# Padding the contraction of two transform stages to 128 rows in a Fourier mixing and two-layer kernel

## The chip, the core and the metric

One core of a Trainium2 chip runs the whole program. The metric is the device time of one execution in microseconds (us); the lower the better. Five engines work side by side: TensorE (PE; its weight loads are listed apart as PEld), VectorE (DVE), ScalarE (ACT), GpSimd (POOL) and SyncE (SP), which here only issues transfers. A matmul on PE multiplies a stationary tile (rows x up to 128 columns, loaded by a weight load) with a moving tile (the same rows x the columns streamed, at most 512 here); "94*128 94x512" in the profile means 94 rows by 128 stationary columns, with 512 columns streamed.

## The reference

The first half is a Fourier mixing along the sequence of 3008 positions, the second a two-layer network with a leaky rectifier. Shapes: x is 8 x 3008 x 256, the filters 1505 x 256, the two weights 256 x 2048 and 2048 x 256.

```python
X = np.fft.rfft(x, axis=1)
Y = X * (filt_r + 1j * filt_i)[None, :, :]
y = np.fft.irfft(Y, n=x.shape[1], axis=1)      # 8 x 3008 x 256
t = y.reshape(8 * 3008, 256)
h = t @ w_in
out = np.maximum(0.01 * h, h) @ w_out          # 24064 x 256, float32
```

## The kernel before

**The transform.** A sequence of 3008 is taken as 94 x 32 (`N1`, `N2`). For one batch there are four stages, each a set of matmuls in fp16 with sums in fp32 in PSUM:

- stage 1 (`s1_group`, line 259): a transform of length 94 along `n1`. The stationary tile is `fwd1` (94 of its 128 rows are in use, the rest are zero), the moving tile two of the 32 columns `n2` of `x_sb`, each with 256 channels: 16 matmuls of 94 rows x 512 columns for one batch. `x_sb` has 128 partitions; its rows 94 and up hold nothing that the transform needs. A load of x writes 96 rows (`R1`), in the last batch 94.
- stage 2 (`s2_group`, line 308) and the products with the filter (lines 314 to 323), which run on DVE and POOL; on the way the two halves of the partitions are swapped by transfers on SP's queue (lines 318 and 319).
- stage 3 (`sa_group`, line 330): the first inverse stage, 12 matmuls of 128 rows x 512 columns for one batch.
- stage 4 (`sb_group`, line 351): the inverse along `n1`. The stationary tile is `z2`, the moving tile a slice of the constant `i1_sb` with 94 columns. Both have `K4` = 96 rows in use. One batch takes 16 groups of four matmuls with 96 rows x 94 columns; ACT copies each group into `yt` (line 341).

Between stages 1 and 2 and between 3 and 4 the data is turned by way of DRAM (`dz1`, `dz2`): a store from `st1` or `st2`, a load into `z1` or `z2` (`t1_load`, `t2_load`). `z1`, `z2`, `st1` and `st2` are halves of the large tiles `big[1]` and `big[2]`, so rows 96 to 127 of `z2` keep what an earlier use of `big[1]` left there.

**The first batch** goes another way: its stages are written out as a list of steps in the string `FIRST` (the helpers `s1p`, `s2p`, `sap`, `sbp` and others), its stage 1 is line 379 and its stage 4 line 442, and turns are done by transposes on DVE. `xc` (`round_x`, line 464) rounds the first six columns of x, which come by an early load in fp32, into `x_sb`. `warm` issues matmuls on an idle tile (line 373).

**The network.** The 24064 tokens go in 47 chunks of 512. The first layer (`moe1`, line 514) and its rectifier on ACT (line 519) are followed one chunk later by the second layer: the first three chunks as plain matmuls (line 681), the others in seven products of half-size blocks with sums of blocks on DVE (lines 555 and 589 and the functions around them).

**The order.** It is fixed when the program is built. Each piece of work has a due time in units of half of a pair of first-layer matmuls (`at`, `plan`, the tables `PLANS`, `AFTER`, `REST`, `DUE`), and a heap issues the pieces in that order; stages 1 to 4 of batches 1 to 7 are put between the network's matmuls of earlier batches. Semaphores make each instruction wait for what it reads and for what it overwrites.

**Constants.** `_build_np_constants` makes the transform matrices on the host; they are stored with the program and loaded. `i1_sb` is loaded twice: for the first batch with one layout (`i1_d`, 128 rows), and from about 82 us on with the layout of the other batches (`i1t_d`, 96 rows, line 719 on SP's queue).

Of the kernel before, what the change touches and what calls it, by code (L numbers as in the profile page):

```python
# [11 lines left out]
P = 128  # L12
# [7 lines left out]
N1, N2 = 94, 32  # L20
NC = 24
Q = 32
R1 = 96
# [3 lines left out]
def _build_np_constants(N):  # L27
    n1, n2 = np.arange(N1), np.arange(N2)
    h = N2 // 2

    k2 = np.concatenate([np.arange(h), np.arange(N2 - 1, h - 1, -1)])

    sg = np.where(k2 < h, 1.0, -1.0)[None, :]
    th = 2 * np.pi * np.outer(n2, k2) / N2
    co, si = np.cos(th), np.sin(th)

    fwd1 = np.zeros((P, P))
    fwd2 = np.zeros((P, NC, P))
    inv1 = np.zeros((P, N2, N1))
    inv2 = np.zeros((P, P))  # L40

    for s, (qr, qi) in enumerate(((0, 2), (1, 3))):
        k1 = NC * s + np.arange(NC)

        cr, ci = (slice(64 * i + s, 64 * i + 64, 2) for i in range(2))
        r, i = (slice(Q * q, Q * q + Q) for q in (qr, qi))
        ang = 2 * np.pi * np.outer(n1, k1) / N1
        fwd1[:N1, qr * Q : qr * Q + NC] = np.cos(ang)
        fwd1[:N1, qi * Q : qi * Q + NC] = -np.sin(ang)
        for c in range(NC):  # L50
            t = th + 2 * np.pi * n2[:, None] * k1[c] / N
            fwd2[r, c, cr], fwd2[i, c, cr] = np.cos(t), np.sin(t)
            fwd2[r, c, ci], fwd2[i, c, ci] = -np.sin(t) * sg, np.cos(t) * sg

        w = np.where((k1 == 0) | (k1 == N1 // 2), 1.0, 2.0)[:, None] / N1
        for j in n2:
            t = ang.T + 2 * np.pi * j * k1[:, None] / N
            inv1[qr * Q : qr * Q + NC, j, :] = w * np.cos(t)
            inv1[qi * Q : qi * Q + NC, j, :] = -w * np.sin(t)
        inv2[cr, r], inv2[ci, r] = co.T, -(si * sg).T  # L60
        inv2[cr, i], inv2[ci, i] = si.T, (co * sg).T
    inv2 /= N2


    inv2r = np.concatenate([inv2[:64], -inv2[:64]], axis=0)
    inv2i = np.concatenate([inv2[64:], inv2[64:]], axis=0)
    small = np.stack([fwd1, inv2, inv2r, inv2i], axis=1)

    fwd2t = fwd2.reshape(4, Q, NC, P).transpose(1, 0, 2, 3).reshape(P, NC, P)
    inv1t = inv1.reshape(4, Q, N2, N1)[:, :NC].transpose(1, 0, 2, 3).reshape(4 * NC, N2, N1)  # L70
    fwd2 = fwd2.reshape(P, FP, NC // FP, P).transpose(1, 0, 2, 3)
    return tuple(np.ascontiguousarray(t).astype(np.float16) for t in (fwd2, inv1, small, fwd2t, inv1t))

# [2 lines left out]
def kernel(  # L76
# [9 lines left out]
    nc = tc.nc  # L86
    B, N, D = x.shape
# [30 lines left out]
    )  # L118

    f2_np, i1_np, small_np, f2t_np, i1t_np = _build_np_constants(N)  # L120
    f2_d = nc.inline_tensor(f2_np, name="fwd2_const")
    i1_d = nc.inline_tensor(i1_np, name="inv1_const")
    small_d = nc.inline_tensor(small_np, name="small_const")
    f2t_d = nc.inline_tensor(f2t_np, name="fwd2t_const")
    i1t_d = nc.inline_tensor(i1t_np, name="inv1t_const")
# [3 lines left out]
    i1_sb = cpool.tile([P, N2, N1], FP16, name="i1_sb")  # L129
# [6 lines left out]
    x_sb = cpool.tile([P, N2, D], FP16, name="x_sb")  # L136
# [19 lines left out]
    def bank(kind, n, w, hold=0.75):  # L156
        if kind == "ph":
            t = wide[turn[kind] % 2]
            turn[kind] += 1
        else:  # L160
            i = min(range(len(single)), key=lambda i: frees[i])
            t, frees[i] = single[i], max(frees[i], clock["now"]) + hold
        return t[:, : n * w].rearrange("p (n w) -> p n w", n=n)
# [5 lines left out]
    def at(time, f):  # L169
        clock["n"] += 1  # L170
        heapq.heappush(work, (time, clock["n"], f))
# [4 lines left out]
    def need(*what):  # L176
        for w in what:
            assert w in issued, w

    def noted(what, f):  # L180
        f()
        issued.add(what)

    def soon(delay, f):
        at(clock["now"] + delay, f)
# [3 lines left out]
    fwd1, inv2, inv2r, inv2i = (small_sb[:, i, :] for i in range(4))  # L189
# [47 lines left out]
    K4 = 4 * NC  # L237
# [9 lines left out]
    def ring(t, half):  # L247
        v = t[:, ts(half, Q * D // 2)].rearrange("p (r n d) -> p r n d", r=4, n=4)
        return [v[:, r] for r in range(4)]

    z1, z2 = ring(big[1], 0), ring(big[1], 1)
    st1, st2, st1_more = ring(big[2], 0), ring(big[2], 1), ring(big[1], 1)

    def s1_group(b, g, copy):
        def go():
            ps = bank("pf", 2, D)
            h = g // 2
            need(("x", b, h if b > 1 else 0), *[("st1", b, h - 4)] * (h > 3 and b > 1))
            nc.tensor.matmul(ps, fwd1[:N1], x_sb[:N1, ds(2 * g, 2), :], start=True, stop=True)  # L259
            issued.add(("s1", b, g))  # L260
            st = st1[h % 4] if b > 1 or h < 4 else st1_more[h % 4]
            copy(st[:, ds(2 * (g % 2), 2), :], ps)  # L262
            if g % 2:
                soon(AFTER[0], lambda: noted(("st1", b, h), lambda: nc.sync.dma_start(
                    dz1[b % 2][ds(4 * h, 4)].rearrange("n p d -> p n d"), st)))
        return go
# [71 lines left out]
    def quad_copy(h, dt, ps, copy):  # L338

        yv = yt[:, dt, ts(h, QT)].rearrange("p (a c) -> p a c", c=4)  # L340
        copy(yv, ps.rearrange("p c a -> p a c"))  # L341

    def sb_group(b, g, copy):
        h, dt = g // 2, g % 2

        def go():
            ps = bank("pf", 4, N1)
            need(("z2", b, h), ("i1t",))
            issued.add(("sb", b, g))
            for j in range(4):  # L350
                nc.tensor.matmul(ps[:, j, :], z2[h % 4][:K4, j, ts(dt, P)], i1_sb[:K4, 4 * h + j, :],  # L351
                                 start=True, stop=True)
            quad_copy(h, dt, ps, copy)
        return go
# [108 lines left out]
    def round_x(n0, n, e):  # L463
        engine[e](x_sb[:N1, ds(n0, n), :], x_early[:N1, ds(n0, n), :])

    FIRST = """
        xc 0 4 A, xc 4 2 D, warm 18, s1p 0 0 4 b3, s1p 0 4 2 b0, warm 3, s1p 0 14 2 b1, s1e 0 4 2 D,
        s1e 0 0 4 A, s1p 0 10 4 b4, s1e 0 10 4 A, s1p 0 6 4 b3, s1e 0 14 2 D, warm 4, s1p 0 20 4 b4,
        s1e 0 6 4 D, s1p 0 16 4 b3, s1e 0 16 4 A, s1p 0 26 2 b2, s1p 0 24 2 b0, s1e 0 24 2 A, s1e 0 20 4 D,
        s1p 0 28 2 b1, s1p 0 30 2 b4, s1e 0 26 2 D, s1e 0 30 2 A, s1e 0 28 2 D, t1 0, t1 1, warm 14,  # L470
# [12 lines left out]
        sbe 0 3 D, sbe 1 0 D  # L483
    """
    steps = dict(s1p=s1p, s1e=s1e, t1=t1, s2p=s2p, s2d=s2d, s2a=s2a, s2m=s2m, sap=sap, sae=sae, t2=t2,
                 sbp=sbp, sbe=sbe, x=load_x, w_out=load_w_out, xc=round_x, warm=keep_warm)
    for step in FIRST.split(","):
        what, *args = step.split()
        steps[what](*(int(v) if v.isdigit() else v for v in args))
# [226 lines left out]
                lambda v=k1s: dve(fa_sb[64:P, v], fa_sb[0:64, v]))):  # L716
            at(TWICE[0] + TWICE[1] * (3 * i + n), f)
    at(F2T, lambda: noted(("f2t",), lambda: nc.sync.dma_start(f2_sb[:], f2t_d.ap())))
    at(26, lambda: noted(("i1t",), lambda: nc.sync.dma_start(i1_sb[:K4], i1t_d.ap())))
    for b in range(1, B):  # L720
        z = 47 * (b - 4) if b > 4 else 0
        p = PLANS[min(b, 4) - 1]
# [18 lines left out]
    while queue:  # L741
        time, n, stage, b, g, f = heapq.heappop(queue)
# [62 lines left out]
```

## Time and profile before

| What | Value |
|---|---|
| runs | 746.96, 747.57, 748.95 us; median 747.57 |
| span of the profiled execution (first to last instruction) | 745.2 us |
| PE busy, share of the span | 738.0 us, 99% |
| granted TensorE clock, mean | 0.999 |
| matmuls of line 259 (stage 1, batches 1 to 7) | 112, from 35.1 to 508.2 us |
| matmuls of line 351 (stage 4, batches 1 to 7) | 448, from 109.2 to 711.0 us |
| matmuls in all | 8017 |
| load of `i1t_d` (line 719) | one, 564 KB, issued at 82.1 us |

The program's own time is known only by the runs; the span is what the profiler saw of one execution. A busy PE says little by itself, since matmuls overlap in the array: the mean duration of one is a latency, and what counts for a stream of them is the step from the start of one to the start of the next.

### The profile page before, as it was taken

How to read it: one execution, taken by the hardware profiler on the slowest of the kernel's cores; microseconds unless marked ns; L12 is line 12 of the kernel's file. 1: busy time of each engine (PE TensorE's matmuls, PEld its weight loads, DVE VectorE, ACT ScalarE, POOL GpSimd, SP SyncE). 2: the span in 40 equal slices, each digit the busy share in tenths (PEclk: the TensorE clock that was granted, in tenths of full speed). 3: DMA queues.
4: the chain of work that ended last, by engine and by line, in shares of the span. 5: the costliest groups of instructions: out<-in, count | busy, mean ns of one | idle time of the engine just before them, and what ended most of it. 6: DMA issues, size and time to landing. Idle time of an engine off the chain costs nothing.

```text
span 745.2 us, 19416 instructions
## 1 busy us (share of the span) xinstructions
PE 738.0 (99%) x8017; PEld 528.9 (71%) x8017; DVE 504.6 (68%) x686; ACT 559.1 (75%) x755; POOL 166.2 (22%) x171
## 2 busy tenths in 40 slices
PE   9999999999999999999999999999999999999997
PEld 3556667677687777877778777777777777777776
DVE  5987637766776766766777667766677676465566
ACT  4776787888878787877777787787777777777762
POOL 6503412332232212121232222121212210000000
PEclk9999999999999999999999999999999999999999
DMA  9997797888876666655675656543554333111012
GB/s 207 229 224 197 191 224 216 209 195 208 216 181 147 159 186 176 169 138 163 193 178 150 159 155 175 156 139 109 144 160 119 106 103 103 60 55 55 29 46 70
DMA packets 119848, 113.64 MB, mean 152 GB/s; under 512 B 16384, under 2 KB 93056, under 8 KB 119568
## 3 DMA queue, kind: packets, MB, share of 16 engines
q1 hardware_dynamic: 104425, 94.73, 42.9%
q0 software_dynamic: 15056, 17.49, 15.8%
q8 instruction: 62, 1.02, 0.6%
q14 instruction: 26, 0.21, 0.1%
q10 hardware_dynamic: 279, 0.19, 0.1%
HBM read 57.51 MB, written 50.33 MB: 145 GB/s over the span
## 4 chain that ended last, share of the span: by engine, by line
PE 96%; DMA 1%; DVE 1%; ACT 1%; issue 0%; ACTq 0%; DVEq 0%
PE ph L514 43%; PE pf L589 18%; PE po_ps L589 18%; PE pf L259 3%; PE pf L351 3%; PE pf L308 2%; PE pf L330 2%; PE po_ps L373 1%; PE pf L681 1%; PE po_ps L681 1%; DMA dz<-big 1%; DMA big<-dz 0%; ACT yt L341 0%; PE pf L442 0%; PE ph L401 0%
## 5 line engine op out<-in xcount | busy, mean ns | idle before, releaser
L519 ACT ACTIVATE gt_c<-ph 128x1024 f16<-128x1024 f32 x376 | 385.3, 1025 | 133.5 <-PE ph L514 122.8
L514 PE MATMUL ph<-yt,w_in_sb 128*128 128x512 f16 (+7 forms) x1728 | 447.3, 351 | 0.2 <-ACT yt L341 0.2
L589 PEld LDWEIGHTS <-gt_c 128*128 128x128 f16 x2800 | 202.2, 98 | 91.1
L323 POOL TENSOR_TENSOR y_b_g<-p_b_g,p_b_g 128x512 f16<-128x512 f32 x84 | 116.4, 1388 | 414.9 <-DMA p_b_g<-p_b_g 249.9
L589 PEld LDWEIGHTS <-big 128*128 128x128 f16 x2128 | 151.2, 98 | 61.4
L514 PEld LDWEIGHTS <-w_in_sb 128*128 128x128 f16 x1728 | 137.5, 98 | 19.7 <-DVE yt L341 0.4
L317 DVE TENSOR_TENSOR p_b_g<-pf,fb_sb 128x512 f32<-128x512 f32 x78 | 53.7, 688 | 31.0 <-PE pf L308 13.8
L589 PE MATMUL po_ps<-wt_sb,gt_c 128*128 128x128 f16 x704 | 70.0, 219 | 0.0
L589 PE MATMUL pf<-wt_sb,gt_c 128*128 128x128 f16 x688 | 68.4, 219 | 0.0
L589 PE MATMUL pf<-w_out_sb,gt_c 128*128 128x128 f16 x720 | 67.9, 219 | 0.0
L589 PE MATMUL pf<-wt_sb,big 128*128 128x128 f16 x704 | 67.2, 219 | 0.0
L262 ACT CAST big<-pf 128x512 f16<-128x512 f32 x98 | 57.1, 588 | 11.9 <-PE pf L259 10.5
L589 PE MATMUL po_ps<-w_out_sb,gt_c 128*128 128x128 f16 x688 | 66.0, 219 | 0.0
L589 PE MATMUL po_ps<-wt_sb,big 128*128 128x128 f16 x688 | 65.3, 219 | 0.0
L341 ACT CAST yt<-pf 128x376 f16<-128x376 f32 x120 | 56.4, 473 | 10.9 <-PE pf L351 8.0
L555 DVE TENSOR_TENSOR big<-gt_c 128x2048 f16<-128x2048 f16 (+1 forms) x46 | 58.7, 1276 | 0.1
L555 DVE TENSOR_TENSOR gt_c<-gt_c 128x2048 f16<-128x2048 f16 x43 | 57.4, 1335 | 1.0
L320 DVE TENSOR_TENSOR p_b_g<-pf,fa_sb 128x512 f32<-128x512 f32 x84 | 57.2, 681 | 0.2
L555 DVE TENSOR_TENSOR big<-gt_c,big 128x2048 f16<-128x2048 f16 (+1 forms) x45 | 55.3, 1230 | 0.0
L555 DVE TENSOR_TENSOR big<-big,gt_c 128x2048 f16<-128x2048 f16 (+1 forms) x45 | 55.2, 1227 | 0.1
L332 ACT CAST big<-pf 128x512 f16<-128x512 f32 x84 | 49.0, 584 | 4.9 <-PE pf L330 3.0
L259 PE MATMUL pf<-x_sb,small_sb 94*128 94x512 f16 x109 | 41.6, 381 | 0.0
(97 smaller groups left out, 625.9 us busy)
## 6 DMA issues: line engine op xcount, KB each, us to landing
dz<-big SPq DMA_DIRECT2D x98, 256.0 KB
p_b_g<-p_b_g SPq DMA_DIRECT2D x156, 128.0 KB
out_dram<-ost_c_h SPq DMA_DIRECT2D x118, 128.0 KB
big<-dz SPq DMA_DIRECT2D x42, 256.0 KB
big<-dz SPq DMA_DIRECT2D x56, 192.0 KB
x_sb<-in_x_dram POOLq DMA_DIRECT2D x40, 192.0 KB, 4.4
x_sb<-in_x_dram POOLq DMA_DIRECT2D x2, 768.0 KB, 9.1
w_in_sb<-in_moe_w_in_dram POOLq DMA_DIRECT2D x1, 1024.0 KB, 13.2
```

Of the source, the lines that this page charges most:

```text
L259: nc.tensor.matmul(ps, fwd1[:N1], x_sb[:N1, ds(2 * g, 2), :], start=True, stop=True)
L262: copy(st[:, ds(2 * (g % 2), 2), :], ps)
L317: nc.vector.tensor_tensor(p2[:], ps, fb, AL.mult)
L320: nc.vector.tensor_tensor(p1[:], ps, fa, AL.mult)
L323: ("y", b, g), lambda: nc.gpsimd.tensor_tensor(y1[:], p1[:], p3[:], AL.add)))
L332: nc.scalar.copy(st2[h % 4][:, ds(2 * (g % 2), 2), :], ps)
L341: copy(yv, ps.rearrange("p c a -> p a c"))
L351: nc.tensor.matmul(ps[:, j, :], z2[h % 4][:K4, j, ts(dt, P)], i1_sb[:K4, 4 * h + j, :], start=True, stop=True)
L514: nc.tensor.matmul(ph[:, j, ds(t - ci * CH, e - t)], w_in_sb[:, dt, ts(ct, P)], yt[:, dt, ds(t % N, e - t)], start=(dt == 0), stop=(dt == ...
L519: nc.scalar.activation(gts[ci][:, ds(2 * g, 2), :], ph, AF.Lrelu)
L555: nc.vector.tensor_tensor(*(v[:, ds(c0, n)] for v in (o, i0, i1)), op)
L589: nc.tensor.matmul(of[t], a()[:, c, ts(t, P)], w[:, c, :], start=(c == 0), stop=(c == NCH - 1))
```

## The change

Stages 1 and 4 of batches 1 to 7 use all 128 rows of their tiles. `fwd1` has zero rows from 94 on already; the constant `inv1t` is built with zero rows from 96 on and its load brings all 128 rows. Where one factor's rows are zero, the other's must be finite: rows 96 to 127 of `x_sb` are set to zero by four memsets on DVE at the start (`blank`, 32 rows x 8 columns x 256 channels each), and rows 94 and 95 hold what the loads brought. Rows 96 to 127 of `z2` keep what was there. The first batch's own steps (lines 379 and 442) are as before.

```diff
@@ in _build_np_constants
-    inv1t = inv1.reshape(4, Q, N2, N1)[:, :NC].transpose(1, 0, 2, 3).reshape(4 * NC, N2, N1)
+    inv1t = np.zeros((P, N2, N1))
+    inv1t[: 4 * NC] = inv1.reshape(4, Q, N2, N1)[:, :NC].transpose(1, 0, 2, 3).reshape(4 * NC, N2, N1)
@@ in s1_group
-            nc.tensor.matmul(ps, fwd1[:N1], x_sb[:N1, ds(2 * g, 2), :], start=True, stop=True)
+            nc.tensor.matmul(ps, fwd1, x_sb[:, ds(2 * g, 2), :], start=True, stop=True)
@@ in sb_group
-                nc.tensor.matmul(ps[:, j, :], z2[h % 4][:K4, j, ts(dt, P)], i1_sb[:K4, 4 * h + j, :],
+                nc.tensor.matmul(ps[:, j, :], z2[h % 4][:, j, ts(dt, P)], i1_sb[:, 4 * h + j, :],
                                  start=True, stop=True)
@@ after round_x
+    def blank(i):
+        nc.vector.memset(x_sb[R1:P, ts(i, N2 // 4), :], 0.0)
+
     FIRST = """
-        xc 0 4 A, xc 4 2 D, warm 18, s1p 0 0 4 b3, s1p 0 4 2 b0, warm 3, s1p 0 14 2 b1, s1e 0 4 2 D,
+        blank 0, blank 1, blank 2, xc 0 4 A, xc 4 2 D, blank 3, warm 18, s1p 0 0 4 b3, s1p 0 4 2 b0, warm 3, s1p 0 14 2 b1, s1e 0 4 2 D,
@@ the load of the constant
-    at(26, lambda: noted(("i1t",), lambda: nc.sync.dma_start(i1_sb[:K4], i1t_d.ap())))
+    at(26, lambda: noted(("i1t",), lambda: nc.sync.dma_start(i1_sb[:], i1t_d.ap())))
```

More of the change, by code (lines that the diff above doesn't have):

```diff
@@ L485 @@
     steps = dict(s1p=s1p, s1e=s1e, t1=t1, s2p=s2p, s2d=s2d, s2a=s2a, s2m=s2m, sap=sap, sae=sae, t2=t2,
-                 sbp=sbp, sbe=sbe, x=load_x, w_out=load_w_out, xc=round_x, warm=keep_warm)
+                 sbp=sbp, sbe=sbe, x=load_x, w_out=load_w_out, xc=round_x, warm=keep_warm, blank=blank)
     for step in FIRST.split(","):
```

## The prediction, made before the changed kernel ran

> **What bounds the kernel now.** I read the page's busy times and its chain of waits first, then the matmul groups kept apart by shape, then the starts of single matmuls.
>
> ```profile
> PE 738.0 (99%) x8017; PEld 528.9 (71%) x8017; DVE 504.6 (68%) x686; ACT 559.1 (75%) x755; POOL 166.2 (22%) x171
> PE 96%; DMA 1%; DVE 1%; ACT 1%; issue 0%; ACTq 0%; DVEq 0%
> 120.00:720.00 600.00, 600.00 (x6752) 1.00 0.54 144
> ```
>
> The first line gives busy time by engine, the second the shares of the chain that ended last, the third (busy time of PE by stretches) says that from 120 to 720 us PE was busy for 600.00 of 600.00 us at full granted clock. So in that stretch the time is the sum of the steps from one matmul's start to the next; no other engine's time counts unless it makes PE wait. What the change touches there are two groups, beside a full-row one of the same width as the first:
>
> ```profile
> L259 PE MATMUL pf<-x_sb,small_sb 94*128 94x512 f16 x109 | 41.6, 381 | 0.0
> L259 PE MATMUL po_ps<-x_sb,small_sb 94*128 94x512 f16 x3 | 1.1, 379 | 0.0
> L351 PE MATMUL pf<-i_sb,big 96*128 96x94 f16 x448 | 38.1, 206 | 0.2 <-DMA big<-dz 0.2
> L330 PE MATMUL pf<-y_b_g,small_sb 128*128 128x512 f16 x84 | 31.8, 379 | 0.0
> ```
>
> The mean durations (381, 206, 379 ns) are latencies and overlap their neighbours, so they do not price anything. The price is the step, taken from the matmul start times in this trace (medians over matmuls that did not wait, ns from a start to the next start):
>
> ```
> full 128 rows, columns streamed:  64: 28.3   128: 55.9   192: 82.6   256: 109.2   320: 135.8   384: 162.7   448: 189.5   512: 216
> L259 (94 rows, 512), after a 128-row matmul:      220     the 128-column matmul behind it: 58 (undisturbed: 56)
> L330 (128 rows, 512), after a 128-row matmul:     216     the 128-column matmul behind it: 56
> L351 (96 rows, 94), first to fourth of a group:   45.7, 44.4, 44.4, 44.3     the 128-column matmul behind them: 58
> L379 (94 rows, 512), three in a row at 7.66 us:   220, 215, 215     then L373 with 128 rows: 220, 215, 215
> ```
>
> The reader should see that a matmul whose row count differs from the one before it takes some 4 ns more than its width says, that the way back costs some 2.6 ns (5 for the 512-wide L373), and that matmuls within a run of 94 rows cost nothing extra (215). Full-row steps lie on a straight line in the columns, 0.417 ns each.
>
> **The change part by part.** The order of instructions is the same on every engine, except for four memsets more on DVE; the waits are on the same engines and queues.
>
> *L259, 112 matmuls (16 in each of seven batches).* Each stands alone between full-row matmuls. Averaged over all that did not wait, the excess is 4.1 ns on its own step and 2.6 on the next. With 128 rows it is an L330: no excess. Gain 112 x 6.7 ns = 0.75 us. Bounds: 0.75, and 0 if the excess is not due to the row count.
>
> *L351, 448 matmuls in 112 groups of four.* The way back to 128 rows: 112 x 2.6 = 0.29 us. In the group, 45.7 + 44.4 + 44.4 + 44.3 = 178.8 ns. No row shows 94 columns over full rows at full width. The line of full-row widths gives 55.9 - 34 x 0.417 = 41.7 ns, so 166.8 for four: 12.0 ns x 112 = 1.34 us. This is one end. The other: 94 columns cost 44.4 whatever the rows, and only the first step's 1.3 ns goes: 0.15 us. For the first end speaks that all eight full-row widths lie on the line within 1 ns, that the excess is the same for all 32 places in i1_sb (44 to 46 ns), so not a matter of where the 94 columns start, and that the two groups that PE entered after waiting (at 109.2 and 130.5 us) made their first step in 41 and 40 ns: 94 columns can pass in 41.7. Against it speaks that L379's 94-row steps within a run show no excess, so fewer rows alone are not slow. I take the line, the nearest row for a full-row matmul, and keep 0.15 for the range.
>
> *The rows added.* The loads of the stationary side last 98 ns for 94, 96 and 128 rows alike; all lie under matmuls. The Trainium skill, in "TensorE: Matmul & The Clock Gate", section "Step-by-step: what each phase is for", says that a weight load's time follows the number of columns and that the row count does not matter. The load durations agree. By that rule alone nothing would be gained by the padding, and the time would stay at 747.6; the starts behind a change of rows speak against it.
>
> *Four memsets on DVE at the start,* 32 rows x 1024 words each. The nearest row is the memset of the same length at 1.34 us:
>
> ```profile
> 1.34 0.91 DVE L234 MEMSET big<- 128x1024 uint32 x1 [0.20 <-issue]
> 6.07 0.42 DVE L464 CAST x_sb<-big 94x512 f16<-94x512 f32 x1 [3.82 <-DMA big<-in_x_dram]
> 8.51 0.69 DVE L288 CAST big<-pf 128x512 f16<-128x512 f32 x1 [2.01 <-PE pf L379]
> ```
>
> In the timeline (start, duration, idle time before it) DVE sits idle for 3.82 us until the first input lands, and 2.01 us behind the cast. Three memsets take 3 x 0.91 = 2.73 us, or 3 x 1.09 by the other memset (0.27 for 256 words): they end between 5.0 and 5.5, before 6.07. The fourth ends by 7.6, before 8.51. Cost 0. If the cover were gone, the cast would be late; what waits for it is the third L379 matmul, at 8.09, 1.6 us after the cast's end, so up to 1.6 us of overrun costs nothing either.
>
> *The constant's load* (line 719, issued once on SP's queue) grows from 564 to 752 KB. The queue's next entries:
>
> ```profile
> 82.14 0.59 SPq L719 DMA_DIRECT2D i_sb<-inv1t_const  x1
> 85.75 1.76 SPq L575 DMA_DIRECT2D out_dram<-ost_c_t  x2
> 87.64 0.53 SPq L318 DMA_DIRECT2D p_b_g<-p_b_g  x1
> ```
>
> 188 KB at the 218 GB/s that the core moved from 80 to 120 us is 0.9 us of transfer; SP issues nothing until 85.75, and the first use is at 109.2. Should it delay the swap at 87.64 by all of the 0.9 us, the sum on POOL behind it has spare time: in that batch the sums end 3.8 to 10.3 us before PE reads them. Cost 0; without that cover 0.9 us.
>
> **Sum.** 0.75 + 0.29 + 1.34 = 2.38 us off the span, 745.2 to 742.8. The median of the runs is 747.57, 2.4 us above the span of the profiled execution; I keep that part: 747.57 - 2.38 = **745.2 us**.
>
> **The rivals.**
>
> *A, the 94 columns keep their 44.4 ns.* Gain 0.75 + 0.29 + 0.15 = 1.19: **746.4**. For it: no slow steps inside L379's runs. Against: the 40 and 41 ns after waits. Only two such steps, so nearly as likely.
>
> *B, the rows are not the cause* (what the change says does not happen on the array): the excess belongs to changing stationary tiles or buffers, and stays. **747.6**. Against: L330 and L308 change tile and buffer as well and show none.
>
> *C, slower: full-row matmuls with 94 columns run as line 442's do.* Those are the only ones in the trace (first batch, 64-column stationary halves):
>
> ```profile
> L442 PE MATMUL pf<-i_sb,big 128*64 128x94 f16 x96 | 4.9, 241 | 0.2 <-DVE big L434 0.2
> L401 PE MATMUL ph<-big,f_sb 128*64 128x128 f16 x72 | 3.0, 221 | 0.0
> ```
>
> In its group at about 64 us the pairs start some 60 to 65 ns apart, slower than the 58 mean of line 401's pairs, which are wider. If L351 took 60 instead of the 44.4 of now, it would lose 448 x 15.6 = 7.0 us, less the 1.04 us of the row changes: **753.5**. It decides against the change as soon as a step costs over 2.3 ns more than now. Against it: line 442's weights are strided and load in 157 ns where the others take 98, and the pairs follow the loads.
>
> *D, the memsets hold up POOL's transfers.* POOL writes its transfers' lists from 1.24 to 6.19 us; if it stood still for the 2.7 us of three memsets, the filter, complete at 17.33, would come at 20.1, 1.2 us after DVE's first product with it (18.86), and PE's line 425 later by as much: 1.2 us lost. With A's gain 747.6. The Trainium skill ("SBUF — State Buffer", "SBUF: two separate sides") warns that some vector instructions lock POOL out of writing descriptors. This trace shows no lock under a memset: the x load issued at 1.91, inside the 0.91 us memset of 1.34, took 0.53 us, the next one, at 2.42 without a memset, 0.52.
>
> **How the numbers follow.** Forecast 0.45, A 0.37, B 0.08, C 0.05, D 0.03, other 0.02. The three runs before span 2.0 us, so a median can be off by about 0.8; 0.3% (2.24 us) is about what can be told from no change, and the forecast's 2.38 lies hardly beyond it. Faster by more than 0.3%: 0.6 of the forecast, a tenth of A, 0.31 in all; slower: C and some of the rest, 0.06; within: 0.63. The range runs from 744.3 (forecast less 0.9) over A to 747.7, which takes in B and D; C is left out.
>
> **What would show it.** In the changed trace: the step of the L259 matmul 216 and the one behind it 56; L351's four at 41.7 (the forecast) or 44.4 (A), 60 (C), and 56 behind them; the memsets done before 6.07 and PE's wait-free stretch unchanged. The forecast is wrong if L351's step stays above 43, or if PE waits anew before 120 us.

## The result and the profile after

| | before | changed |
|---|---|---|
| median of 22 runs each | 747.58 us | 746.70 us |
| ratio changed to before | | 0.9986, 95% interval 0.998 to 0.9991 |
| span of the profiled execution | 745.2 us | 744.2 us |

The change saves 1.05 us by the ratio (0.67 to 1.50 by its interval), 0.14%: a gain clear of no change, and under half of the 2.38 us that were forecast. The time lies within the stated range (744.3 to 747.7 us) and next to rival A's 746.4, but not for A's reason, as the experiments show.

The page of the changed kernel, busy times and the chain that ended last:

```profile
PE 737.1 (99%) x8017; PEld 528.4 (71%) x8017; DVE 506.5 (68%) x690; ACT 558.9 (75%) x755; POOL 167.2 (22%) x171
PE 98%; DVE 1%; ACT 0%; issue 0%; DVEq 0%; ACTq 0%
```

PE's busy time by stretches (length, busy us, matmuls, granted clock, DMA share, GB/s):

```profile
80.00:120.00 40.00, 40.00 (x370) 1.00 0.88 221
120.00:720.00 600.00, 600.00 (x6764) 1.00 0.55 144
```

The matmul groups that were changed (busy us, mean ns of one | idle time before them):

```profile
L260 PE MATMUL pf<-x_sb,small_sb 128*128 128x512 f16 x109 | 41.3, 379 | 0.0
L352 PE MATMUL pf<-i_sb,big 128*128 128x94 f16 x448 | 37.8, 206 | 0.0
```

PE is still the bound and busy for all of the 600 us; the same 600 us now hold 12 matmuls more (6764 against 6752). The means hardly differ (379 for 381, 206 for 206), as they are latencies. The gain shows only in the starts. For each changed matmul or group the next table follows 14 steps, start to start, and gives how far each is from what its width says (columns / 2.4 + 2.5 ns, the line through the steps of the full-row matmuls: 55.9 ns for 128 columns, 216 for 512); means over the 68 to 112 places after 85 us where PE did not wait and no other changed matmul was near:

```
excess in ns                  step 0     1      2      3      4      5      6      7     sum of 14
stage 1, before (94 rows)       4.17   2.62  -0.82  -0.86  -0.78   0.00   0.11  -0.13      4.35
stage 1, changed                0.05  -0.05  -0.03   0.04  -0.05   0.02  -0.04   0.05      0.00
stage 4, before (96 rows)       4.12   2.60   2.74   2.62   2.64  -0.85  -0.84  -0.69     12.34
stage 4, changed               -0.85   4.99   2.78   2.56  -0.83  -0.85  -0.66   0.05      7.19
```

For stage 1, step 0 is the changed matmul and step 1 the one behind it; for stage 4, steps 0 to 3 are the group and step 4 the matmul behind it. Two things are to be seen. First, a stall is partly made good: the three steps behind it are 0.7 to 0.9 ns short, so a stage-1 matmul cost 4.35 ns net, not 6.7. Second, padding clears stage 1 altogether but stage 4 only in part: its first step is now free, its second is slower than before, its third and fourth are as they were.

Net, the steps give 112 x 4.35 = 0.49 us for stage 1 and 112 x (12.34 - 7.19) = 0.58 us for stage 4, together 1.06 us (with rounding): what the runs show. That the two spans differ by nearly the same, 1.04 us, is partly chance, since two other differences between the profiles cancel. The first stage-1 matmul of the first batch started 0.4 us later in the changed kernel (8.05 against 7.66 us): the warm-up matmuls ahead of it, 512 columns wide, step by 0.427 us at first and then by 0.216, which is read here as the rise of PE's clock, and that came two slow matmuls later (at 7.40 instead of 6.58 us). And PE's waits after 84 us were 0.36 us shorter (0.10 against 0.46); a wait is counted here where a step is over 20 ns longer than its width says, by what it is longer. Both vary from profile to profile of one and the same kernel, as is seen below.

DVE's timeline at the start of the changed kernel (start, duration, idle before it and what ended it):

```profile
1.34 0.91 DVE L235 MEMSET big<- 128x1024 uint32 x1 [0.20 <-issue]
2.50 0.91 DVE L468 MEMSET x_sb<- 32x1024 uint32 x1 [0.25 <-issue]
3.58 0.91 DVE L468 MEMSET x_sb<- 32x1024 uint32 x1 [0.16 <-issue]
4.65 0.91 DVE L468 MEMSET x_sb<- 32x1024 uint32 x1 [0.16 <-issue]
6.76 0.42 DVE L465 CAST x_sb<-big 94x512 f16<-94x512 f32 x1 [1.19 <-DMA big<-in_x_dram]
7.45 0.91 DVE L468 MEMSET x_sb<- 32x1024 uint32 x1 [0.27 <-issue]
8.90 0.69 DVE L289 CAST big<-pf 128x512 f16<-128x512 f32 x1 [0.54 <-PE pf L380]
```

Each memset takes 0.91 us; three are done at 5.56, and DVE still waits 1.19 us for the first input. The fourth ends at 8.36, 0.54 us before DVE has its next input. SP's queue around the larger constant; its next issue comes 3.65 us after the constant's (3.61 before):

```profile
82.39 0.56 SPq L723 DMA_DIRECT2D i_sb<-inv1t_const  x1
86.04 1.76 SPq L579 DMA_DIRECT2D out_dram<-ost_c_t  x2
87.93 0.53 SPq L319 DMA_DIRECT2D p_b_g<-p_b_g  x1
```

### The profile page after: what moved, and what is told of

The parts are those of the page before. It is cut to its first block, busy times and chain, and to the rows that moved or that the text cites. A ratio compares the mean times of both kernels' runs of the same rounds, so it can differ in the third digit from the quotient of the medians.

```text
span 744.2 us, 19420 instructions
## 1 busy us (share of the span) xinstructions
PE 737.1 (99%) x8017; PEld 528.4 (71%) x8017; DVE 506.5 (68%) x690; ACT 558.9 (75%) x755; POOL 167.2 (22%) x171
## 4 chain that ended last, share of the span: by engine, by line
PE 98%; DVE 1%; ACT 0%; issue 0%; DVEq 0%; ACTq 0%
PE ph L518 44%; PE pf L593 18%; PE po_ps L593 18%; PE pf L260 3%; PE pf L352 3%; PE pf L309 2%; PE pf L331 2%; PE po_ps L374 2%; PE pf L685 1%; PE po_ps L685 1%; ACT yt L342 0%; PE pf L443 0%; PE ph L402 0%; PE pf L426 0%; DVE big L289 0%; DVE big L435 0%
## 5 line engine op out<-in xcount | busy, mean ns | idle before, releaser
L559 DVE TENSOR_TENSOR big<-gt_c 128x2048 f16<-128x2048 f16 (+1 forms) x46 | 57.2, 1244 | 0.1
L260 PE MATMUL pf<-x_sb,small_sb 128*128 128x512 f16 x109 | 41.3, 379 | 0.0
```

Source lines behind the costliest of these rows:

```text
L260: nc.tensor.matmul(ps, fwd1, x_sb[:, ds(2 * g, 2), :], start=True, stop=True)
L559: nc.vector.tensor_tensor(*(v[:, ds(c0, n)] for v in (o, i0, i1)), op)
```

## The experiments

Expectations and tables below give steps, start to start, as means over the undisturbed matmuls of that profile; "behind" is the matmul that follows.

**One part of the change alone.** `only_s1` keeps the memsets and the stage-1 line and takes the stage-4 part back; `only_sb` is the kernel before with the stage-4 line and the padded constant, without memsets; `blanks_only` is the kernel before with the memsets alone. (Only the lines that matter are shown.)

```diff
# only_s1, against the changed kernel (and the constant and its load as before)
-  nc.tensor.matmul(ps[:, j, :], z2[h % 4][:, j, ts(dt, P)], i1_sb[:, 4 * h + j, :],
+  nc.tensor.matmul(ps[:, j, :], z2[h % 4][:K4, j, ts(dt, P)], i1_sb[:K4, 4 * h + j, :],
# only_sb, against the changed kernel (and no memsets)
-  nc.tensor.matmul(ps, fwd1, x_sb[:, ds(2 * g, 2), :], start=True, stop=True)
+  nc.tensor.matmul(ps, fwd1[:N1], x_sb[:N1, ds(2 * g, 2), :], start=True, stop=True)
# blanks_only: both lines, the constant and its load as before
```

> The change in stage 1 alone (with the four memsets; stage 4 with 96 rows as before). Theory (the cost belongs to each change of the row count): the stage-1 matmul steps 216 ns instead of 220 and the one behind it 56 instead of 58; stage 4 as before, 45.7 / 44.4 / 44.4 / 44.3 and 58 behind. Span about 0.75 us below before in the part after the start. Rival (the two stages help each other, the gain needs both): stage 1 still 220 or its gain under 0.4 us. Start: if the memsets held the first input or the clock back, the first stage-1 matmul of the first batch starts at about 8.05 us as in the changed kernel; if that was chance, at 7.66 or 8.05 without order.

> The change in stage 4 alone, no memsets, stage 1 with 94 rows as before. Theory: the four steps of stage 4 are 40.8 / 46.7 / 44.4 / 44.2 and the matmul behind them 55, together 6.1 ns a group less, 0.69 us over 112 groups; stage 1 still 220 and 58. Start: without the memsets the first stage-1 matmul of the first batch starts at 7.66 if the memsets were the cause of 8.05 in the changed kernel.

> The kernel before with the four memsets and nothing else (they fill rows that nothing reads). Theory: all steps as before, memsets of 0.91 us done before the first input lands, start of the first stage-1 matmul between 7.3 and 8.1 us following the rise of the clock. Rival (the memsets delay the first input): that cast starts 0.4 us or more later than in the kernels without them (6.07 and 6.63 us so far).

```
                stage 1, excess behind   stage 4, steps of a group    excess behind   waits after 84 us   span    run
before          220.0   2.6              45.7  44.4  44.4  44.3        2.6             0.46               745.2   
only_s1         215.8   0.0              45.7  44.4  44.5  44.2        2.5             0.93               745.3   747.26
only_sb         220.0   2.6              40.9  46.9  44.5  44.2       -0.9             0.48               744.7   746.90
blanks_only     220.0   2.6              45.7  44.4  44.5  44.3        2.6             0.22               745.7   747.71
changed         215.9  -0.1              40.8  46.7  44.5  44.2       -0.9             0.10               744.2
```

The two parts are independent: each shows exactly its own steps. The span of `only_s1` is not below that of before all the same, where some 0.75 us less was expected: the 0.49 us were taken up by waits 0.47 us longer and a first stage-1 matmul 0.18 us later (7.84 against 7.66). A single execution can't show a gain of this size; the steps can. The 0.69 us expected of `only_sb` left out the steps that catch up, as the forecast did. (The run of before beside the first two took 747.31, the 21 beside `blanks_only` had a median of 747.83.)

*The start.* Over all profiles, the first stage-1 matmul of the first batch started at 7.37 to 7.77 us in the four kernels without memsets (before, `only_sb`, and two below) and at 7.36 to 8.05 in the ten with them. The steps of the warm-up matmuls fell to 0.216 us anywhere from 4.40 to 7.40 us. The memsets have no cost there that could be told from this scatter. The first input's cast on DVE began at 5.86 to 6.63 without and 6.10 to 6.76 with them; a delay of some 0.2 us in that landing is not excluded. It would cost time only where the warm-up ends early: in six of the fourteen profiles (one without memsets, five with) the step into that first stage-1 matmul was 0.3 to 1.2 us longer than 0.216 us, and in the others it was not.

**Is it any change of the row count?** `s1_96rows` is the kernel before with 96 rows instead of 94 in stage 1.

```diff
-  nc.tensor.matmul(ps, fwd1[:N1], x_sb[:N1, ds(2 * g, 2), :], start=True, stop=True)
+  nc.tensor.matmul(ps, fwd1[:R1], x_sb[:R1, ds(2 * g, 2), :], start=True, stop=True)
```

> The kernel before with 96 rows instead of 94 in stage 1 (rows 94 and 95 of fwd1 are zero). Theory T (any row count other than that of the neighbours costs): 220 and 58 as with 94. Rival U (only a number of rows that is not a multiple of 32 costs): 216 and 56, and 0.75 us less, with stage 4's 45.7 first step then to be put down to something else.

The step is 220.0 and the excess behind it 2.6, as with 94 rows (span 745.4, one run 747.50): theory T. A multiple of 32 doesn't help; of the counts tried (94, 96, 128), only that of the neighbours is free.

**What keeps stage 4's second to fourth step slow.** The constant's slices are 94 columns of 2 bytes, 188 bytes apart, and so is their start address. Counted from the start of `i1_sb`, the first of a group of four starts at a multiple of 752 bytes, and so of 16; the others start 12, 8 and 4 bytes past one. `stride96` stores them 192 bytes apart and still streams 94; `stride104` 208 bytes apart; `psum128` leaves the constant and puts the four outputs 512 instead of 376 bytes apart.

```diff
# stride96, against the changed kernel (stride104 with 104; the constants padded alike, line 442's slice cut to :N1)
-    i1_sb = cpool.tile([P, N2, N1], FP16, name="i1_sb")
+    i1_sb = cpool.tile([P, N2, R1], FP16, name="i1_sb")
-                nc.tensor.matmul(ps[:, j, :], z2[h % 4][:, j, ts(dt, P)], i1_sb[:, 4 * h + j, :],
+                nc.tensor.matmul(ps[:, j, :], z2[h % 4][:, j, ts(dt, P)], i1_sb[:, 4 * h + j, :N1],
# psum128, against the changed kernel
-            ps = bank("pf", 4, N1)
+            ps = bank("pf", 4, P)[:, :, :N1]
```

> The changed kernel with the constant of stage 4 stored 96 columns apart instead of 94 (94 are still streamed), so each moving slice starts at a multiple of 192 bytes. Theory P (the 94-column step is slow where the moving slice starts off a round address): steps of 41 to 42 ns for all four, some 9 ns a group less, 1.0 us in all. Rival Q (it is where the sums are written in PSUM, 376 bytes apart) and rival R (it is the number 94 itself, or the chain of weight loads): steps stay 40.8 / 46.7 / 44.4 / 44.2.

> The changed kernel with the four outputs of a stage-4 group 128 columns (512 bytes) apart in PSUM instead of 94 (376 bytes); ACT still copies 94 columns of each. Theory P (moving slice's address): steps stay 40.8 / 46.7 / 44.4 / 44.2. Rival Q (address in PSUM): 41 to 42 for all four, 1.0 us less in all. Rival R (the number of columns, or weight loads): no change.

> The changed kernel with the moving slices 104 columns (208 bytes) apart: multiples of 16 bytes, of 32 only every second, of 64 only every fourth. If a start at a multiple of 16 bytes is enough: 41 / 41 / 41 / 42 as with 192 bytes. If 32 or 64 are needed: the second and fourth step (32), or the second to fourth (64), stay at 44 to 47.

```
             steps of a stage-4 group    excess behind   span    run
changed      40.8  46.7  44.5  44.2      -0.9            744.2
psum128      40.8  46.7  44.4  44.2      -0.9            743.8   745.78
stride96     40.8  40.9  40.8  41.7       2.4            743.3   745.30
stride104    40.9  40.9  40.9  41.6       2.5            744.6   746.50
```

Theory P holds: it is where the moving slice starts. A multiple of 16 bytes is enough, as `stride104` shows, and one of 8 is not, as the third place in `changed` shows. Where the sums go does not matter, and 94 columns in themselves are not slow: rival A's premise falls. In `stride96` the 14 steps of a group add up to -0.02 ns of excess, from 7.19. The Trainium skill says in "SBUF — State Buffer", section "Specifications (TRN2)", that SBUF has lines of 16 bytes and that each crossing to a new one pays a penalty; the grain of 16 bytes agrees with these steps. How many such lines a slice touches does not tell its cost, though: the 188 bytes of the fourth place, from 4 bytes past a line's start, touch 12 lines, as those of the first place do, and are slow.

**Both costs in one group.** `before_stride96` is the kernel before, 94 and 96 rows, with the slices 192 bytes apart.

> The kernel before (96 rows in stage 4, 94 in stage 1), with the constant's slices 192 bytes apart. Theory (row change and slice address are two costs that hide each other in a group's first step): first step 45 to 46 as before for the change of rows, the other three 41 to 42, and 58 behind. Rival (with 96 rows the 44.4 came from the rows): the three stay at 44.4.

The steps are 45.7 / 40.9 / 40.9 / 40.8, with an excess of 4.3 behind (span 744.4, one run 746.56). So in the kernel before the change of rows was the whole excess of the first step and the slice address that of the other three. The 14 steps add up to 3.97 ns of excess a group, against 12.34 in the kernel before. By these sums aligning the slices alone would have been worth 112 x 8.37 ns = 0.94 us, more than the padding of stage 4 (0.58).

**Does the further gain reach the time?** `stride96_t` is `stride96`, timed; `cols96` streams 96 columns, the last two zeros; `after_again` is the changed kernel once more, timed; `later` is `stride96` with the first two stage-4 groups of batch 1 a little later.

```diff
# cols96, against stride96 (and the copy takes 94 of the 96)
-            ps = bank("pf", 4, N1)
+            ps = bank("pf", 4, R1)
-  ... i1_sb[:, 4 * h + j, :N1],
+  ... i1_sb[:, 4 * h + j, :],
# later, against stride96
-                behind += READ
+                behind += READ + (0.8 if stage == 4 and b == 1 and g < 4 else 0)
```

> The changed kernel with the moving slices of stage 4 at multiples of 192 bytes, timed. By the steps of its first profile: 6.7 ns for each of 112 stage-1 matmuls, and per stage-4 group 178.8 + 2.6 before against 164.1 + 2.4, 14.9 ns, so 0.75 + 1.67 = 2.4 us less than before, ratio 0.9968. Rival (as PE gets earlier it only waits longer for the loads of z2): under 1.2 us, ratio above 0.9984.

> As stride96, and 96 columns streamed, two of them zeros that nobody copies. If an odd width costs something of its own: the step is 42.5 by the line of full-row widths, and the matmul behind the group has no excess, 4 x 42.5 = 170 against 164.1 + 2.4 with 94 streamed: 0.4 us slower than stride96, within the noise of the times. If the excess behind the group (2.4 ns) is not of the width: 172.4, 0.7 us slower. Ratio to before 0.997 to 0.998.

> stride96 with one thing more: the first two stage-4 groups of the first planned batch stand 13 matmuls (some 1.2 us) later in PE's order, all else unchanged. Theory W (part of the gain is lost in a wait of PE for the first load of z2 at about 110 us, 0 to 1.5 us long from run to run): the wait there is under 0.3 us in the profile, and the median is 0.3 to 0.8 us below that of stride96, ratio to before about 0.998. Rival (the wait is a matter of a single profile, and the gain is lost elsewhere, for one in steps that run longer in some executions): median as stride96, ratio 0.9986.

> The changed kernel again, beside the others on the same chip: ratio 0.9986, steps of stage 4 40.8 / 46.7 / 44.4 / 44.2 and 55 behind as in its first profile. Start: if the memsets delay it, the first stage-1 matmul of the first batch starts at about 8.05 again; if the time at which PE's clock rises sets it, anywhere from 7.3 to 8.1, later where the clock rises later. Wait at about 110 us: 0 again if the change removes it, 0 to 1.5 us if it is chance.

```
               median of runs     ratio to before, interval     waits after 84 us in the profile
after_again    746.35  (n 11)     0.9985  0.9976 to 0.9994      0.57
stride96_t     746.43  (n 11)     0.9986  0.9978 to 0.9995      1.58   (stride96: 0.10)
cols96         746.54  (n 12)     0.9991  0.9981 to 1.0         0.65
later          746.80  (n 11)     0.9985  0.9976 to 0.9993      0.88
```

The changed kernel's gain repeats. In this second profile PE waited 0.15 us at about 109 us, and the first stage-1 matmul of the first batch started at 7.82 us: so the 0 and the 8.05 us of the first profile do not belong to the change. `cols96` has steps of 42.5 for all four and no excess behind them, as expected; the uneven 40.8 to 41.7 and the 2.4 behind in `stride96` belong to the width of 94 and add up to nothing. None of these beats the changed kernel beyond the intervals. For `stride96_t` that is less than its steps give: 1.06 + 112 x 7.19 ns = 1.87 us net, where its interval allows 0.37 to 1.64 (the expectation of 2.4 was made without the steps that catch up, and was too high by that). By that interval at least 0.2 us is lost. One place where it can be lost is seen in its profile, PE's timeline (start, duration, and in brackets the idle time before, which leaves out what the modelled end of the matmul ahead covers, and what ended it):

```profile
108.15 0.59 PE L519 MATMUL ph<-yt,w_in_sb 128*128 128x512 f16 x2
108.58 0.22 PE L594 MATMUL po_ps<-wt_sb,gt_c 128*128 128x128 f16 x1
110.11 0.34 PE L353 MATMUL pf<-i_sb,big 128*128 128x94 f16 x4 [1.31 <-DMA big<-dz]
```

and SP's queue ahead of it in the same profile:

```profile
100.43 0.58 SPq L336 DMA_DIRECT2D dz<-big  x1
103.24 0.36 SPq L266 DMA_DIRECT2D dz<-big  x1
107.29 1.75 SPq L280 DMA_DIRECT2D big<-dz  x4
```

The first stage-4 group of batch 1 waits for its load of `z2`, which waits for the last store of stage 3 to land in DRAM: issued at 100.43, followed by the load at 107.29, 6.86 us later. In the changed kernel's first profile the same store was issued at 100.96 and the load at 106.42, 5.46 us, and PE did not wait. Over all other profiles this took 5.1 to 6.0 us, and PE waited 0 to 0.5 us here. `later` took that wait away and got another: the layer's matmul that reads the newest `yt` then stood waiting for ACT's copy.

```profile
111.36 0.57 PE L519 MATMUL ph<-yt,w_in_sb 128*128 128x448 f16 x3
112.44 0.19 PE L519 MATMUL ph<-yt,w_in_sb 128*128 128x64 f16 x1 [0.51 <-ACT yt L343]
```

Its ratio came out as the rival expected (0.9985), but as one wait was traded for another, moving these groups does not answer whether such waits take the gain of `stride96`. The single runs suggest that only some executions lose it: the fastest runs of `stride96_t`, `cols96` and `later` took 745.36, 745.12 and 745.32 us, below all 33 runs of the changed kernel (746.20 to 748.05 and 745.98 to 747.00), and their slowest 748.18, 749.07 and 748.37 us, above all of them (the sets did not all run on one chip). Over the fourteen profiles PE's waits after 84 us range from 0.10 to 1.58 us, and the same kernel has had both ends (`stride96`); whether they grow as PE gets faster stays open.

## Why the prediction came out as it did

**Bound and place: right.** PE's steps set the time, apart from waits of 0.1 to 0.5 us after 84 us before and after; the order of PE's matmuls is the same in both kernels, and in the changed kernel's profile nothing that was added on DVE and SP made PE wait.

**Stage 1: the mechanism was right, the size was not.** The steps went from 220 to 216 and from 58 to 56, as forecast, and `s1_96rows` and `only_s1` show that it is the change of the row count. The term "112 x 6.7 ns = 0.75 us" counted only the two slow steps. The three behind them were 2.5 ns short in sum, and that went too: 4.35 ns net, 0.49 us. A sign of it stood in the prediction's own rows: the 215 ns behind L379's 220 are below the 216 of an undisturbed step.

**Stage 4: the step that failed is "I take the line, the nearest row for a full-row matmul".** The forecast had four steps of 41.7 and 1.34 us, plus 0.29 for the way back. Measured were 40.8, 46.7, 44.5 and 44.2, and an excess of -0.9 behind; net 0.58 us for both terms. By the prediction's own sign (a step of L351 above 43) the forecast was wrong here. The row count cost only the first step and the way back. The other three were slow because their slices start off a multiple of 16 bytes, which the padding does not touch. The prediction had ruled the start address out, since the excess was "the same for all 32 places". That comparison was blind: every fourth place, the only kind at a multiple of 16, was also the first of its group and carried the cost of the row change, and the other 24 are all off. The 40 and 41 ns after a wait, which it read as a sign that 94 columns can pass in 41.7, were both first places: the right conclusion on the width, and a sign of the address that was not read.

**Rival A** named a gain of 1.19 us, near to the 1.05, and three of the four steps did stay at 44 ns or more; but its reason (94 columns take 44.4 whatever the rows) is refuted by `stride96` and `stride104`. Its 0.75 us for stage 1 was 0.26 too much, as it lacked the catch-up, and its 0.44 for stage 4 was 0.14 too little: that the sum came out so near is in part luck. **Rival B** is refuted by `only_s1`: the excess goes with the rows. The rule of the Trainium skill that was weighed under "The rows added", in "TensorE: Matmul & The Clock Gate", section "Step-by-step: what each phase is for", is true of the weight loads (98 ns before and after) and does not tell the step. **Rival C** did not come: the slowest full-row step was 46.7, not 60. **Rival D** did not come: POOL's first eight issues took as long as before and came at the same times; the ninth came at 9.12 instead of 8.20 us, released by an x load that landed later, and no PE wait followed from it.

**The edits costed at nothing** were covered as said: the first three memsets were done at 5.56 against 5.0 to 5.5 forecast (0.16 to 0.25 us passes ahead of each, which the sum left out), and the first use of the constant came without a wait.

## What to carry to other kernels

Where PE is busy without a gap, read the step from start to start, for the operation and for some ten steps behind it: a stall of 6.7 ns was 4.35 net. Keep the row count of neighbouring matmuls equal by padding with zeros, and start every moving slice at a multiple of 16 bytes (shown here for slices of 94 columns of 2 bytes): by the steps each was worth 4 to 7 ns for a matmul or a group of four here, so it pays only where there are many of them, and the gain of the second was not seen in the medians. Before ruling out a cause because all cases look alike, look whether the one case that differs is hidden by another cost.

## What the runs showed of the hardware that was not expected

- Behind a stall of a few ns the next three steps are 0.7 to 0.9 ns shorter than the steady 55.8 or 215.8 ns.
- A step whose moving slice starts off a multiple of 16 bytes takes 44.2 to 46.7 ns for 94 columns, against 40.8 to 41.7 where it starts at one; the place of the output in PSUM made no difference.
- The same store to DRAM at about 100 us was followed by its dependent load 5.1 to 6.0 us later in thirteen profiles and 6.9 in one, where PE lost 1.47 us by it, and the first stage-1 matmul started anywhere from 7.36 to 8.05 us, as the warm-up steps fell from 0.427 to 0.216 us at 4.4 to 7.4 us: scatter of the size of the whole gain of the change.
